# Loading v of row 1 earlier and placing row 1's values in the middle of chunk 0's second product

## The chip, the cores and the metric

The kernel runs on one core of a Trainium2 chip. The metric is the device time of one execution in microseconds (us). Three runs of the kernel before gave 306.92, 307.39 and 307.52; the median is 307.39. The profiled execution took 307.2 us, of which the span from the first to the last instruction is 305.4.

The engines named here are PE (TensorE: matmuls and transposes into PSUM), ACT (ScalarE), DVE (VectorE), POOL (GpSimd) and SP (SyncE, which only issues transfers). A transfer is issued by an engine and moved by the core's 16 DMA engines. Queue 0 of the profile carries what POOL issues, queue 1 what SP issues.

## What is computed

The program is windowed attention over 8 batches ("rows" in the kernel) with 8 heads each, followed by a feed-forward layer over all 4608 tokens.

```python
# q, k, v: (8, 8, 576, 64) float32;  w_in: (512, 2048);  w_out: (2048, 512)
scores = q @ k^T / 8
# heads 0-3 ("sliding"): key j is seen by query i if 0 <= i - j < 32
# heads 4-7 ("dilated"): 0 <= i - j < 128 and (i - j) % 4 == 0
attn = softmax(masked scores)
x = (attn @ v), heads side by side            # (4608, 512)
out = relu(x @ w_in) ** 2 @ w_out             # (4608, 512) float32
```

## The kernel before

The kernel interleaves two streams on PE. The feed-forward layer works on nine chunks of 512 tokens. Attention works on eight rows of 576 tokens and writes its result, transposed, into `xT`. While chunk c is multiplied, row c+1 goes through attention. The chunks are generators, and `pump(n)` lets the current one emit n further steps (two matmuls of the first product, and two matmuls of 512 columns in chunk 0's second product, or four or eight matmuls of 256 columns in the later ones). Between two calls of `pump` stands a piece of attention. Every engine executes its own instructions in the order in which they were written down, so the places of the `pump` calls decide what stands beside what.

Row 0 and the masks come first, together with short matmuls on zeros. Then these loads are issued for what follows. `landed` is a one-column copy on POOL that holds everything behind it on POOL until a transfer has arrived.

```python
load_w_out(0, 1)
landed(wi[:, NDM - 1, 1023:1024])
nc.gpsimd.memset(sq[:, :, :, 0:1], 0.0)
load_sliding_qk(1)              # SP: q, k of row 1, heads 0-3
load_dilated_qk(1)              # POOL: q, k of row 1, heads 4-7
load_w_out(1, 4)                # POOL: the other three quarters of w_out
landed(wo[:, 3, DM - 1 :])
nc.gpsimd.memset(sv[:, :, :, 0:1], 0.0)
nc.gpsimd.memset(sd[:, :, :, 0:1], 0.0)
load_v(1)                       # SP: six transfers into sv, two into sd
landed(wo[:, NFF - 1, DM - 1 :])
landed(sd[:, 1, HH - 1, DIL * D - 1 :])
dk = keep_qk(2)                 # POOL: q, k of row 2, DRAM to DRAM, to fp16
```

`keep_qk` writes row 2's q and k as fp16 into a DRAM tensor `dk`; later DMA transposes read it into `QKTx` and `QKTd`. Rows 2 to 7 get q and k in this way, row 1 through PE transposes (`pt`, `pd`).

Chunk 0 then goes through its two products. The second one goes four output tiles wide (`po_0` to `po_3`), a quarter of w_out at a time:

```python
g0 = hidden(0)
pending.append(mm1_gen(0, g0))
pump(28)
cast_sliding_qk(1, (nc.scalar, nc.vector, nc.scalar, nc.vector))
pump(1000)
pending.append(mm2_by_rows_gen(0, g0))
pump(1)
for hp in range(2):
    for i in (1, 0):
        t_sliding(1, hp, i, True)     # 6 transposes (pt) and a copy
        pump(1)
    if hp:
        for g in range(2):
            s_sliding(1, g)           # 12 score matmuls (ps), 2 exp, 2 masks
            pump(2)
for g in range(2):
    for i in (1, 0):
        t_dilated(1, g, i, True)      # 6 transposes (pd) and two copies
        pump(1)
scores_dilated(1, lambda: pump(3))    # twice: 16 score matmuls (pz), 2 exp, 2 masks
cast_v(nc.scalar)                     # ACT: sv -> vp, then sd -> vd (two instructions)
pump(2)
# ... rows_and_load: pump(1); after its second call row 2's DMA transposes and v
attn_values(1, rows_and_load, True)
pump(1000)
```

`attn_values` emits, with a call of its argument after each: three groups of sliding values (`pav`, 8 matmuls, then reciprocal and product on DVE), output transposes `px`, four groups of dilated values (`paw`), and output transposes `py`; the transposes are copied by ACT into `xT`. All of row 1's `pt`, `ps`, `pd`, `pz`, `pav`, `paw`, `px` and `py` tiles take turns in one PSUM pool of two buffers:

```python
papool = ctx.enter_context(tc.tile_pool(name="papool", bufs=2, space=bass.MemoryType.PSUM))
```

For rows 2 to 7 the loop over `b` emits chunk b-1 with row b inside it. In its first round (b = 2) it stores chunk 0, forms sums of w_out on DVE (`weight_sums`), and then:

```python
if b == 2:
    # ... stores of chunk 0
    dk = keep_qk(b + 1)
    for _ in weight_sums():
        pump(2)
    pump(2)
else:
    pump(11)
for g in range(2):
    s_sliding_x(b, g)
    pump(5)
s_dilated(b, 0)
pump(5 if b == 2 else 7)
s_dilated(b, 1)
# ... DMA transposes of row b+1
pump(2 if b == 2 else 6)
cast_v(nc.scalar)
# ... load_v(b + 1)
pump(5 if b == 2 else 3)
n_val[0] = 0
def rows():
    n_val[0] += 1
    pump(1 if b == 2 and n_val[0] > 7 else 2)
attn_values(b, rows)
pump(1000)
```

Of the kernel before, what the change touches and what calls it, by code (L numbers as in the profile page):

```python
# [17 lines left out]
def kernel(  # L18
# [9 lines left out]
    nc = tc.nc  # L28

    B, H, S, D = q.shape  # L30
    W = 32
    DIL = 4
    NTOK, DM = out.shape
    DFF = moe_w_in.shape[1]
    assert (B, H, S, D) == (8, 8, 576, 64) and DM == H * D and NTOK == B * S
    HH = H // 2
    NDM = DM // P
    NFF = DFF // P
# [8 lines left out]
    NB = S // QB  # L47
# [25 lines left out]
    wo = wpool.tile([P, NFF, DM], FP16, name="wo")  # L73
# [9 lines left out]
    sv = stg.tile([P, NB, HH, D], FP32, name="sv")  # L83
    sd = stg.tile([P, 2, HH, DIL * D], FP32, name="sd")
# [13 lines left out]
    def load_sliding_qk(b, engs=(nc.sync, nc.sync)):  # L98
        for i, src in enumerate((q, k)):
            engs[i].dma_start(  # L100
                out=sq[:, i, :, :],
                in_=src[b, 0:HH].rearrange("h (p j) d -> p h (j d)", j=6),
            )
# [17 lines left out]
    def load_sliding_v(b, m0=0, m1=NB):  # L121
        for m in range(m0, m1):
            lo = QB * m - PADP
            p0 = PADP if m == 0 else 0
            nc.sync.dma_start(
                out=sv[p0:P, m, :, :],
                in_=v[b, 0:HH, lo + p0 : lo + P, :].transpose([1, 0, 2]),
            )

    def load_dilated_v(b, eng, ts=(0, 1)):  # L130
        vv = v[b, HH:H].rearrange("h (i c) d -> i h (c d)", c=DIL)
        if 0 in ts:
            eng.dma_start(out=sd[PADD:P, 0, :, :], in_=vv[0:QD])
        if 1 in ts:
            eng.dma_start(out=sd[:, 1, :, :], in_=vv[QD - PADD : CL])

    def load_v(b):
        load_sliding_v(b)
        load_dilated_v(b, nc.sync)

    def load_dilated_qk(b):
        for i, src in ((1, k), (0, q)):
            s4 = src[b, HH:H].rearrange("(g e) (p j) d -> e p g (j d)", e=2, j=12)
            for e in range(2):
                nc.gpsimd.dma_start(out=nd_[48 * e : 48 * (e + 1), i, :, :], in_=s4[e])
# [18 lines left out]
    def copy(eng, o, i):  # L164
        if eng is nc.scalar:
            nc.scalar.copy(o, i)
        else:
            eng.tensor_copy(o, i)
# [26 lines left out]
    def cast_sliding_v(eng, step, m0=0, m1=NB):  # L195
        for m in range(m0, m1, step):
            copy(eng, vp[:, m : m + step, :, 0:D], sv[:, m : m + step, :, :])

    def cast_dilated_v(eng, step, ts=(0, 1)):
        for t in ts:  # L200
            for c in range(0, DIL, step):
                copy(
                    eng,
                    vd[:, t, c : c + step, :, 0:D],
                    sd[:, t, :, D * c : D * (c + step)].rearrange("p h (c d) -> p c h d", d=D),
                )

    def cast_v(eng):
        cast_sliding_v(eng, NB)
        cast_dilated_v(eng, DIL)  # L210
# [331 lines left out]
    def pump(n):  # L542
        for _ in range(n):
            while pending:
                try:
                    next(pending[0])
                    break
                except StopIteration:
                    pending.pop(0)


    def pa(name, dt=FP32):
        return papool.tile([P, 2, 512 if dt == FP32 else 1024], dt, name=name, tag="pa")
# [73 lines left out]
    def softmax(u, ps, mask):  # L627
        nc.scalar.activation(AT[:, u, 0:UW], ps[:, :, 0 : UW // 2], ACTF.Exp, scale=scale)  # L628
        nc.vector.tensor_mul(AT[:, u, 0:UW], AT[:, u, 0:UW], mask)  # L629

    def s_sliding(b, hp):
        tiles = [pa(f"ps{b}_{hp}_{half}") for half in range(2)]
        for half, ps in enumerate(tiles):
            for m3 in range(3):
                m = 3 * half + m3
                for e in range(2):
                    r = slice(D * e, D * (e + 1))
                    nc.tensor.matmul(  # L638
                        ps[:, e, QB * m3 : QB * (m3 + 1)],
                        QKTp[hp][r, 1, QB * m : QB * m + P],  # L640
                        QKTp[hp][r, 0, PADP + QB * m : PADP + QB * (m + 1)],
                        start=True,
                        stop=True,
                    )
        for half, ps in enumerate(tiles):
            softmax(2 * hp + half, ps, maskp)
# [19 lines left out]
    def s_dilated(b, g):  # L666
        tiles = [pa(f"pz{b}_{g}_{h}") for h in range(2)]
        for h, ps in enumerate(tiles):
            for a in range(2):
                for t in range(2):  # L670
                    q0 = KPAD + (2 * g + h) * CL + QD * t
                    for e in range(2):
                        r = slice(D * e, D * (e + 1))
                        n = 2 * a + t
                        nc.tensor.matmul(  # L675
                            ps[:, e, QD * n : QD * (n + 1)],
                            QKTd[r, 1, a, q0 - PADD : q0 - PADD + P],
                            QKTd[r, 0, a, q0 : q0 + QD],
                            start=True,
                            stop=True,  # L680
                        )
        for h, ps in enumerate(tiles):
            softmax(4 + 2 * g + h, ps, maskd)
# [148 lines left out]
    def scores_dilated(b, fill):  # L832
        for g in range(2):
            s_dilated(b, g)
            fill()

    def attn_values(b, fill, wide=False):
        xs = []
        for mp in range(3):
            xs += av_sliding(b, 2 * mp, 2 * mp + 2)  # L840
            fill()
        x_sliding(b, 0, xs, wide)
        fill()
        ys = av_dilated(b, 0, 0)
        fill()
        x_sliding(b, 1, xs, wide)
        fill()
        ys += av_dilated(b, 0, 1)
        fill()
        zs = []  # L850
        for a in range(2):
            zs += av_dilated(b, 1, a)
            fill()
        x_dilated(b, 0, ys, wide)
        fill()
        x_dilated(b, 1, zs, wide)
# [9 lines left out]
    def landed(x):  # L866

        nc.gpsimd.tensor_copy(hold[0 : x.shape[0]], x)
# [57 lines left out]
    landed(wi[:, NDM - 1, 1023:1024])  # L926
    nc.gpsimd.memset(sq[:, :, :, 0:1], 0.0)
    load_sliding_qk(1)
    load_dilated_qk(1)
    load_w_out(1, 4)  # L930
    landed(wo[:, 3, DM - 1 :])
    nc.gpsimd.memset(sv[:, :, :, 0:1], 0.0)
    nc.gpsimd.memset(sd[:, :, :, 0:1], 0.0)
    load_v(1)

    landed(wo[:, NFF - 1, DM - 1 :])
    landed(sd[:, 1, HH - 1, DIL * D - 1 :])
    dk = keep_qk(2)


# [7 lines left out]
    for hp in range(2):  # L948
        for i in (1, 0):
            t_sliding(1, hp, i, True)  # L950
            pump(1)
        if hp:
            for g in range(2):
                s_sliding(1, g)
                pump(2)
    for g in range(2):
        for i in (1, 0):
            t_dilated(1, g, i, True)
            pump(1)
    scores_dilated(1, lambda: pump(3))  # L960
    cast_v(nc.scalar)
    pump(2)
    n_val = [0]

    def reload_v(b):
# [16 lines left out]
    for b in range(2, B):  # L982
        pending.append(moe_gen(b - 1))
        pump(1)
        if b < B - 1:

            for i in range(2):
                nc.gpsimd.tensor_copy(hold, QKTx[:, i, PADP + HH * S - 2 : PADP + HH * S - 1])
                nc.gpsimd.tensor_copy(hold, QKTd[:, i, 1, KPAD + S - 1 :])
        if 2 < b < B - 1:  # L990
            dk = keep_qk(b + 1)
        if b == 2:
            for rows, ot in late:
                nc.gpsimd.dma_start(out=rows, in_=ot)
            dk = keep_qk(b + 1)
            for _ in weight_sums():
                pump(2)
            pump(2)
        else:
            pump(11)  # L1000
        for g in range(2):
            s_sliding_x(b, g)
            pump(5)
        s_dilated(b, 0)
        pump(5 if b == 2 else 7)
        s_dilated(b, 1)
        if b + 1 < B:
            transpose_by_dma(dk)
        pump(2 if b == 2 else 6)
        cast_v(nc.scalar)  # L1010
        if b + 1 < B:
            load_v(b + 1)
        pump(5 if b == 2 else 3)
        n_val[0] = 0

        def rows():
            n_val[0] += 1
            pump(1 if b == 2 and n_val[0] > 7 else 2)

        attn_values(b, rows)  # L1020
        pump(1000)
    for c in range(B - 1, NTOKC):
        pending.append(moe_gen(c))
# [31 lines left out]
```

The softmax here doesn't subtract the row's maximum and nothing guards it: scores larger than these inputs give would overflow.

## Time and profile before

| What | Value |
|---|---|
| time, median of 3 runs | 307.39 us |
| span of the profiled execution | 305.4 us |
| PE busy | 296.0 us, 97% of the span |
| DVE, ACT, POOL busy | 208.8, 185.0, 47.9 us |
| granted PE clock, mean | 0.999 |
| chunk 0's second product with row 1 | 38.44 to 62.53 us |
| chunk 1 with row 2 | 62.53 to 95.05 us |
| chunk 2 with row 3 | 95.19 to 126.08 us |

The busy time of an engine is the sum of its instructions; matmuls overlap in the array, so a busy PE is not PE at its peak. A line of the timeline gives the start, the time taken, the engine, the line of the kernel, the operation, output and input, and how many instructions are merged; in brackets stand the idle time before it and what ended it. SPq, POOLq and ACTq lines are issues of transfers: their time is that of issuing, not of moving. `L168` and `L166` are copy helpers, so the tiles tell what is copied.

### The profile page before, as it was taken

How to read it: one execution, taken by the hardware profiler on the slowest of the kernel's cores; microseconds unless marked ns; L12 is line 12 of the kernel's file. 1: busy time of each engine (PE TensorE's matmuls, PEld its weight loads, DVE VectorE, ACT ScalarE, POOL GpSimd, SP SyncE). 2: the span in 40 equal slices, each digit the busy share in tenths (PEclk: the TensorE clock that was granted, in tenths of full speed). 3: DMA queues.
4: the chain of work that ended last, by engine and by line, in shares of the span. 5: the costliest groups of instructions: out<-in, count | busy, mean ns of one | idle time of the engine just before them, and what ended most of it. 6: DMA issues, size and time to landing. Idle time of an engine off the chain costs nothing.

```text
span 305.4 us, 7012 instructions
## 1 busy us (share of the span) xinstructions
PE 296.0 (97%) x2898; PEld 192.3 (63%) x2898; DVE 208.8 (68%) x410; ACT 185.0 (61%) x308; POOL 47.9 (16%) x98
## 2 busy tenths in 40 slices
PE   7899999999998999999999999999999999999995
PEld 3675444544785469646974697459745974684484
DVE  4662474769974797679766977697769775834744
ACT  6567776668924893489348943894389536405710
POOL 7546000206004100320032003200100010000000
PEclk9999999999999999999999999999999999999999
DMA  8999996899989999999929983999320012003004
GB/s 176 227 212 232 236 208 145 155 194 208 314 178 251 267 154 178 267 196 197 230 103 205 203 188 126 217 191 205 115 73 0 2 54 85 2 0 137 2 0 138
DMA packets 85615, 47.89 MB, mean 157 GB/s; under 512 B 68112, under 2 KB 82896, under 8 KB 85200
## 3 DMA queue, kind: packets, MB, share of 16 engines
q1 hardware_dynamic: 76688, 27.24, 41.3%
q0 software_dynamic: 8352, 19.80, 29.2%
q8 instruction: 22, 0.36, 0.5%
q10 hardware_dynamic: 544, 0.43, 0.5%
q14 instruction: 9, 0.07, 0.1%
HBM read 39.85 MB, written 16.52 MB: 185 GB/s over the span
## 4 chain that ended last, share of the span: by engine, by line
PE 89%; DMA 3%; DVE 2%; ACT 2%; POOL 2%; issue 1%; ACTq 0%; POOLq 0%
PE ph L388 42%; PE poa L438 9%; PE pob L438 9%; PE pod L438 5%; PE poe L438 4%; PE poc L438 4%; PE po L409 3%; DMA early<-in_q_dram 3%; PE paw L776 2%; PE pav L759 2%; PE pz L675 2%; PE ps L656 1%; PE px L791 1%; PE py L809 1%; POOL early L119 1%; DVE x_d L740 1%
## 5 line engine op out<-in xcount | busy, mean ns | idle before, releaser
L388 PE MATMUL ph<-xT,wi 128*128 128x512 f16 x576 | 129.8, 380 | 0.3 <-ACT xT L815 0.3
L354 ACT ACTIVATE rt<-ph 128x512 f16<-128x512 f32 x144 | 84.9, 601 | 36.8 <-PE ph L388 36.4
L388 PEld LDWEIGHTS <-wi 128*128 128x128 f16 x576 | 54.4, 98 | 62.9 <-issue 0.6
L358 DVE TENSOR_TENSOR g<-rt 128x1024 f16<-128x1024 f16 x63 | 43.5, 691 | 45.5 <-ACT rt L354 45.2
L438 PEld LDWEIGHTS <-sm 128*128 128x128 f16 x512 | 46.8, 98 | 4.8
L438 PEld LDWEIGHTS <-g 128*128 128x128 f16 x384 | 36.0, 98 | 6.9 <-DVE g L356 1.3
L438 PE MATMUL pob<-T,sm 128*128 128x256 f16 x256 | 32.8, 272 | 0.0
L438 PE MATMUL poa<-wo,g 128*128 128x256 f16 x256 | 32.6, 273 | 0.0
L458 POOL DMA_DIRECT2D out_dram<-otl x6 | 4.6, 761 | 148.4 <-DVE otl L493 131.1
L815 ACT COPY xT<-py 128x576 f16<-128x576 f16 x16 | 10.2, 638 | 25.5 <-PE py L809 25.4
L740 DVE TENSOR_TENSOR x_d<-paw,rcp_d 72x512 f16<-72x512 f32 x32 | 22.0, 687 | 1.1
L797 ACT COPY xT<-px 128x576 f16<-128x576 f16 x16 | 10.3, 642 | 14.0 <-PE px L791 14.0
L628 ACT ACTIVATE AT<-pz 128x576 f16<-128x576 f32 x28 | 16.7, 649 | 1.9 <-PE pz L675 1.5
L409 PE MATMUL po<-wo,g 128*128 128x512 f16 x64 | 17.8, 380 | 0.0
L628 ACT ACTIVATE AT<-ps 128x576 f16<-128x576 f32 x28 | 16.7, 650 | 0.8 <-PE ps L638 0.4
L740 DVE TENSOR_TENSOR x_p<-pav,rcp_p 96x512 f16<-96x512 f32 (+1 forms) x24 | 16.2, 676 | 0.8
L735 DVE RECIPROCAL rcp_d<-paw 72x8 f32<-72x8 f32 x32 | 6.3, 198 | 15.1 <-PE paw L776 15.1
L438 PE MATMUL poe<-wo,sm 128*128 128x256 f16 x128 | 16.5, 273 | 0.0
L438 PE MATMUL poc<-T,sm 128*128 128x256 f16 x128 | 16.4, 272 | 0.0
L438 PE MATMUL pod<-T,g 128*128 128x256 f16 x128 | 16.1, 273 | 0.0
L629 DVE TENSOR_TENSOR AT<-AT,maskp 128x576 f16<-128x576 f16 x28 | 12.7, 457 | 2.8 <-ACT AT L628 1.9
L478 ACT COPY otu<-poa 128x512 f32<-128x512 f32 x8 | 4.7, 586 | 16.1 <-PE poa L438 16.1
(120 smaller groups left out, 352.6 us busy)
## 6 DMA issues: line engine op xcount, KB each, us to landing
sv<-in_v_dram SPq DMA_DIRECT2D x40, 128.0 KB, 4.6
sd<-in_v_dram SPq DMA_DIRECT2D x8, 512.0 KB, 6.8
dk<-in_k_dram POOLq DMA_DIRECT2D x12, 288.0 KB, 6.3
dk<-in_q_dram POOLq DMA_DIRECT2D x12, 288.0 KB, 7.8
out_dram<-otl POOLq DMA_DIRECT2D x6, 512.0 KB, 3.3
out_dram<-otu POOLq DMA_DIRECT2D x6, 512.0 KB, 4.6
sd<-in_v_dram SPq DMA_DIRECT2D x8, 288.0 KB
wi<-in_moe_w_in_dram POOLq DMA_DIRECT2D x4, 512.0 KB, 10.6
```

Source lines behind the costliest of these rows:

```text
L354: nc.scalar.activation(rt[:, o, :], ph[:], ACTF.Relu)
L358: nc.vector.tensor_mul(g[:, ffc - 1 : ffc + 1, :], rt, rt)
L388: nc.tensor.matmul(ph, wi[:, dmk, ffc * P : ffc * P + P], xs[:, dmk, :], start=(n == 0), stop=(n == NDM - 1),)
L409: nc.tensor.matmul(po, g[:, ffc, t * P : (t + 1) * P], wo[:, ffc, :], start=(ffc == 0), stop=(ffc == NFF - 1),)
L438: nc.tensor.matmul(acc, lhs[:, k, t * P : (t + 1) * P], rhs[:, k, :], start=(first and k == 0), stop=(k == NK - 1), skip_group_check=True,)
L628: nc.scalar.activation(AT[:, u, 0:UW], ps[:, :, 0 : UW // 2], ACTF.Exp, scale=scale)
L629: nc.vector.tensor_mul(AT[:, u, 0:UW], AT[:, u, 0:UW], mask)
L675: nc.tensor.matmul(ps[:, e, QD * n : QD * (n + 1)], QKTd[r, 1, a, q0 - PADD : q0 - PADD + P], QKTd[r, 0, a, q0 : q0 + QD], start=True, sto ...
L735: nc.vector.reciprocal(rcp[0:w, 0:n], pv[:, :, :, D])
L740: nc.vector.tensor_tensor(out=x[0:w, 0:n], in0=pv[:, :, :, 0:D], in1=rcp[0:w, 0:n].unsqueeze(3).to_broadcast([w, n, HH, D]), op=ALU.mult,)
L797: nc.scalar.copy(xT[:, 0:2, t0 : t0 + 288], px[:, 0:UW].rearrange("x (c t) -> x c t", c=2),)
L815: nc.scalar.copy(xT[:, 2:4, t0 : t0 + 288].rearrange("x c (i r) -> x c i r", r=DIL), py[:, 0:UW].rearrange("x (c r i) -> x c i r", c=2, r= ...
```

## The change

The loads of row 1's v are issued directly behind those of its sliding q and k, on SP. The two waits for w_out, the wait for v, and the two memsets that held v's load are gone, so `keep_qk(2)` follows w_out on POOL without a hold. In chunk 0's second product the fillers between the pieces of row 1's attention are cut, so that its values come in the middle of the product and the rest of the product comes after them; the cast of the sliding v moves ahead of the dilated scores. In chunk 1 the fillers are placed anew around row 2. The purpose is to have the values of row 1, and row 2's transposes behind them, done sooner.

```diff
     load_sliding_qk(1)
+    load_v(1)
     load_dilated_qk(1)
     load_w_out(1, 4)
-    landed(wo[:, 3, DM - 1 :])
-    nc.gpsimd.memset(sv[:, :, :, 0:1], 0.0)
-    nc.gpsimd.memset(sd[:, :, :, 0:1], 0.0)
-    load_v(1)
-
-    landed(wo[:, NFF - 1, DM - 1 :])
-    landed(sd[:, 1, HH - 1, DIL * D - 1 :])
     dk = keep_qk(2)
@@ row 1 in chunk 0's second product
             t_sliding(1, hp, i, True)
             pump(1)
-        if hp:
-            for g in range(2):
-                s_sliding(1, g)
-                pump(2)
+    for g in range(2):
+        s_sliding(1, g)
+        pump(1)
     for g in range(2):
         for i in (1, 0):
             t_dilated(1, g, i, True)
-            pump(1)
-    scores_dilated(1, lambda: pump(3))
-    cast_v(nc.scalar)
-    pump(2)
+    cast_sliding_v(nc.scalar, NB)
+    scores_dilated(1, lambda: pump(1))
+    cast_dilated_v(nc.scalar, DIL)
@@ row 2 in chunk 1, and the later rows
             for _ in weight_sums():
                 pump(2)
-            pump(2)
@@
             s_sliding_x(b, g)
-            pump(5)
+            pump(7 if b == 2 and g else 5)
@@
-        pump(5 if b == 2 else 3)
-        n_val[0] = 0
-
-        def rows():
-            n_val[0] += 1
-            pump(1 if b == 2 and n_val[0] > 7 else 2)
-
-        attn_values(b, rows)
+        pump(4 if b == 2 else 3)
+        attn_values(b, lambda: pump(2))
         pump(1000)
```

In instructions: PE, ACT, DVE and SP execute as many as before, in another order; POOL has five fewer. On PE the order of chunk 0's second product becomes: the first half of it spread over row 1's scores and values as before but more thinly, and after the last output transpose (`py_1`) 26 of its 64 matmuls in one piece. On ACT, `vp<-sv` stands ahead of the four `AT<-pz`, and the four copies of `po` to the output tile follow the copies of `py`. In chunk 1 the last output transpose is followed directly by chunk 2's first matmul, where one half product (8 matmuls) stood between them before.

## Prediction

> **What bounds the kernel now.** I read the page first, then busy time in 10 us stretches, then the timeline of the stage that the diff edits, then the DMA records packet by packet. From the page:
>
> ```profile
> span 305.4 us, 7012 instructions
> ...
> PE 296.0 (97%) x2898; PEld 192.3 (63%) x2898; DVE 208.8 (68%) x410; ACT 185.0 (61%) x308; POOL 47.9 (16%) x98
> ...
> PE 89%; DMA 3%; DVE 2%; ACT 2%; POOL 2%; issue 1%; ACTq 0%; POOLq 0%
> ```
>
> TensorE is the bound: 97% busy and 89% of the chain that ended last. Busy time by stretch (length, then PE, PEld, DVE, ACT, POOL, clock, DMA share, GB/s):
>
> ```profile
> 40.00:50.00 10.00, 9.49 (x107) 4.99 (x107) 5.94 (x14) 6.35 (x13) 0.18 (x1) 1.00 1.09 201
> 50.00:60.00 10.00, 9.46 (x114) 4.87 (x113) 5.97 (x17) 6.79 (x9) 2.18 (x5) 1.00 0.61 122
> 60.00:70.00 10.00, 9.71 (x61) 4.33 (x58) 7.39 (x14) 6.80 (x12) 0.39 (x1) 1.00 1.03 201
> ...
> 90.00:100.00 10.00, 8.74 (x79) 5.37 (x77) 5.92 (x12) 4.11 (x7) 4.02 (x9) 1.00 1.11 265
> ```
>
> Only chunk 0's second product with row 1 (38.4 to 62.5) and the end of chunk 1 (near 93) have gaps; from 100 us PE is full. The busy figure hides part of the gap. Bare costs: 13.81 us for the 64 matmuls of 512 columns of chunk 0's first product, so 0.216 each; a group of six transposes or eight value matmuls takes 0.26 start to start when nothing holds it, a score group of 12 or 16 takes 0.36. The stage is 64 x 0.216 + (8 transpose + 7 value + 4 output-transpose groups) x 0.26 + 4 x 0.36 = 13.8 + 4.9 + 1.4 = 20.2 us. It takes 62.53 - 38.44 = 24.1. So the most that a better order can win here is about 3.9 us, 1.3%. The timeline of the stage:
>
> ```profile
> 35.24 8.90 SPq L125 DMA_DIRECT2D sv<-in_v_dram  x6
> ...
> 44.24 1.81 SPq L133 DMA_DIRECT2D sd<-in_v_dram  x1
> ...
> 48.05 0.70 ACT L166 COPY QKTd<-pd 128x288 f16<-128x288 f16 x2 [0.89 <-PE pd L577]
> ...
> 48.72 1.19 ACT L628 ACTIVATE AT<-pz 128x576 f16<-128x576 f32 x2
> ...
> 51.86 1.47 ACT L166 CAST vp<-sv 128x1536 f16<-128x1536 f32 x1
> ...
> 53.22 2.00 ACT L166 CAST vd<-sd 128x1024 f16<-128x1024 f32 x2
> 53.38 0.42 PE L759 MATMUL pav<-vp,AT 128*128 128x65 f16 x8 [0.25 <-ACT vp L166]
> ...
> 53.54 0.18 POOL L868 COPY hold<-sd 128x1 f32<-128x1 f32 x1 [5.66 <-DMA sd<-in_v_dram]
> 54.03 0.54 POOL L220 DMA_DIRECT2D dk<-in_k_dram  x1 [0.31 <-issue]
> ...
> 62.53 8.36 PE L388 MATMUL ph<-xT,wi 128*128 128x512 f16 x38 [0.29 <-ACT xT L815]
> ```
>
> Here v is cast only after all exponentials of row 1, its load lands by 53.5, and only then do the four dk copies of row 2 begin. Values cost PE a short wait for the cast; the end of the stage waits for the last xT copy.
>
> **What the Trainium skill says.** "DMA: Bandwidth & Descriptors", section "Queues, rings and completion order": each DMA engine goes round robin, packet by packet, between the queues that have work. Counting this trace's records agrees: from 39 to 44 us queue 0 (w_out, 1024 B) moved 149 to 154 packets a us and queue 1 (v, 256 B) 147 to 184, though v got only a fifth of the bytes. Same page, "Issuing engines are not separate DMA queues": issuing from several engines saves only issue time, the transfers interleave. So v on SyncE's queue isn't put ahead of w_out on GpSimd's. "TensorE: Matmul & The Clock Gate", section "Architectural detail": ACT and DVE are strict FIFO, and PE may only pull weight loads ahead. The order of the ACT program therefore decides; in the trace weight loads do start ahead of a held matmul (one value weight load at 52.76, its matmul at 53.38).
>
> **Part 1, the loads.** Issue of v moves from 35.24 to about 24.6, behind q k of row 1 on one queue. But that queue is busy with q k until 35.5 to 36 (packets of 1536 B end there). So v's data start near 36 instead of 38.6: a gain of about 2.5 us, not 11. From 36, w_out has some 1450 packets left; at 150 a us they last to about 45.5, and v gets about 9.5 x 150 = 1430 of its 2944 packets of 256 B (6 tiles) by then. Its 800 packets of 1024 B (sd) stand behind.
>
> **Part 2, dk unheld.** dk's four copies now follow w_out on GpSimd's queue at once and reach the engines near 45.5, just when v had the engines alone before (486, then 904 packets in the two us from 44). dk is 64 packets of 18432 B. In rows 2 to 7, alone, they pass at 11 to 12 a us, 5.5 to 6 us in all. Beside them v is nearly stopped: from 103 to 107 us 44 dk packets went with 154 packets of sd, 3.5 to one. So over dk's 6 to 7 us (45.5 to 52) v gets about 64 x 3.5 = 220 packets; 1290 are left, at 700 to 900 a us 1.7 us. The sv tiles then land at about 53.5 to 54.5 (before: about 48.5), sd at 160 to 215 a us some 4 to 5 us after, near 58.
>
> **Part 3, the order on ACT and PE.** The cast of sv now stands ahead of row 1's four dilated exponentials on ACT. The attention PSUM pool has two buffers, so the second pair of scores needs the first exponential done, and the first value group the third. Also four transpose groups follow each other with no filler matmul, each needing a buffer from a copy. Walk it, from 41.98 which is unchanged. First score pair 42.51, second 43.6 and 44.1; its exponentials end 44.63 and 45.23. Transpose groups pd at 44.75 and 45.3; their copies (DVE after two masks) end 46.57 and 46.45; next two pd 46.6 and 46.9; copies end 47.86 and 48.0. First two pz at 47.9 and 48.1, filler to 48.7. If sv had landed, ACT casts it 48.0 to 49.47 and the exponentials end at 50.07, 50.66, 51.26, 51.85. So pz of the second pair is at 50.1 and 50.7, the first values at 51.35. From there to the last output transpose the steps go at the pace of DVE's 0.20 + 0.69 and of ACT's copies: py of the second half at about 59.8. Then 26 filler matmuls of 0.216 = 5.6, and chunk 1 begins at about 65.7, where before it was 62.5. Order alone: +3.2 us. With sv landing at 54.2 in place of 48.0 everything from the cast on shifts by 6.2 us, as PE has no other work that stands ahead of it: +9.4 in all. The sd cast then comes at 58, about when it lands, so it adds 0 to 1.
>
> **Part 4, chunk 1.** Before: its last output transpose waits for DVE until 94.01, 1.2 us. After: a half product more stands before it, so that wait goes to near 0. But the half product that followed it is gone, and chunk 2's first matmul needs the ACT copy of that transpose; at 61.37 to 62.53 this took 1.16 us, 0.26 of it work, so 0.9 of new wait. Later chunks take 30.9 us each, chunk 1 takes 95.05 - 62.53 = 32.5; I count -0.4 net. The final xT wait of chunk 0 (0.6 us) is already within part 3. Sum: 307.4 + 9.4 - 0.4 = 316.4. Removing five small GpSimd waits is worth nothing by itself, since no PE wait goes through them but those told.
>
> **Rivals.** (a) v gets through. If the copies start later than I think, or share engines evenly by bytes with v, sv lands by 48 to 50, and only the order costs: +3 to +5, 310.5 to 312. For: dk took 8 us rather than 6 at 54, so it is not always greedy. Against: 103 to 107 us. (b) As designed: v is early enough, values come mid product, the fillers at the end hide the last copy, and most of the 3.9 us of gaps goes: 304.5 to 306. For: no xT wait at 62.5, and row 2's transposes earlier. Against: row 2's keys landed at 68.4 and were wanted at 70.8, so that is no wait now; and 26 fillers at the end stand idle where row 1 has gaps. (c) The starved sd adds its own wait after sv: 318 to 320.
>
> **Range and chances.** Main path 316.4 with some 60%, (a) 30%, (b) and (c) the rest; I put the middle at 315.5. The range 309.5 to 319 covers (a)'s upper part and (c). The 2% line above is 313.5, between (a) and the main path: slower 0.65, within 0.33, faster 0.02 (6.1 us is more than all gaps of both stages).
>
> **What would show it.** ACT's cast of sv beginning at 53 to 55 and ended by DMA sv, with PE idle of 6 to 9 us between 45 and 58 while dk's queue is full: right. Cast near 48: part 2 wrong, (a). First matmul of chunk 1 near 71 to 72: sum right; 65 to 66: order alone; before 62.5: (b), part 3 wrong. Chunk 2's first matmul should wait about 0.9 us for the xT copy. Chunks 2 to 8 must keep 30.9 and 26.0 us.

## The result and the profile after

The changed kernel takes 320.69 us (median of four runs, 319.0 to 321.51) against 307.44 us for the kernel before (four runs, 306.92 to 307.52). The ratio is 1.0428, with a 95% interval of 1.0383 to 1.0472: slower by 13.2 us. The prediction had the direction right and was 5.2 us too low; the measured time lies 1.7 us above its range.

From the page of the changed kernel:

```profile
span 319.2 us, 7004 instructions
...
PE 300.5 (94%) x2898; PEld 195.0 (61%) x2898; DVE 208.7 (65%) x410; ACT 185.4 (58%) x308; POOL 46.8 (15%) x93
...
PEclk9999995599999999999999999999999999999999
...
PE 82%; DMA 5%; SPq 5%; ACT 3%; DVE 3%; issue 1%; ACTq 0%
```

The span grew by 13.8 us and PE's busy time by 4.5, though PE executes the same 2898 matmuls: some of them ran more slowly. The row of the granted clock says which: two of its forty slices, from about 48 to 64 us, show half of full speed. In the chain that ended last, 5% is now a DMA and 5% SyncE's queue.

Busy time of the changed kernel by 10 us stretch (length, then PE, PEld, DVE, ACT, POOL, clock, DMA share, GB/s):

```profile
40.00:50.00 10.00, 7.59 (x95) 4.13 (x94) 5.62 (x13) 5.28 (x11) 0.00 (x0) 0.88 1.21 218
50.00:60.00 10.00, 1.44 (x18) 0.81 (x18) 1.33 (x3) 3.63 (x6) 0.00 (x0) 0.50 1.10 200
60.00:70.00 10.00, 9.77 (x97) 5.32 (x95) 6.67 (x19) 3.60 (x6) 0.74 (x4) 0.76 1.05 222
70.00:80.00 10.00, 10.00 (x54) 4.68 (x54) 2.70 (x5) 5.50 (x10) 3.52 (x6) 1.00 0.56 167
```

PE did 1.44 us of work between 50 and 60, where it did 9.46 before. After that it is full again, but until 64.7 us at half clock, so "9.77 busy" is not 9.77 us of progress. The timeline of the changed kernel names the wait:

```profile
24.74 18.60 SPq L125 DMA_DIRECT2D sv<-in_v_dram  x6
...
36.66 0.52 POOL L220 DMA_DIRECT2D dk<-in_q_dram  x1 [0.81 <-DMA early<-in_k_dram]
...
47.33 0.70 ACT L166 COPY QKTd<-pd 128x288 f16<-128x288 f16 x2 [0.76 <-PE pd L577]
...
48.55 1.04 PE L409 MATMUL po<-wo,g 128*128 128x512 f16 x2
...
56.37 1.47 ACT L166 CAST vp<-sv 128x1536 f16<-128x1536 f32 x1 [8.34 <-DMA sv<-in_v_dram]
57.75 2.35 ACT L628 ACTIVATE AT<-pz 128x576 f16<-128x576 f32 x4
58.45 0.96 PE L675 MATMUL pz<-QKTd 64*128 64x72 f16 x16 [8.86 <-ACT AT L628]
```

ACT stood 8.34 us in front of the cast of sv. The exponentials stood behind the cast, and PE's next score groups (`pz`) stood behind those: 8.86 us. Chunk 1 began at 75.90 instead of 62.53, so 13.4 of the 13.8 us are lost by then.

### The profile page after: what moved, and what is told of

Read it like the earlier page. It is cut to its first block, busy times and chain, and to the rows that moved or that the text cites. A ratio compares the mean times of both kernels' runs of the same rounds, so it can differ in the third digit from the quotient of the medians.

```text
span 319.2 us, 7004 instructions
## 1 busy us (share of the span) xinstructions
PE 300.5 (94%) x2898; PEld 195.0 (61%) x2898; DVE 208.7 (65%) x410; ACT 185.4 (58%) x308; POOL 46.8 (15%) x93
## 4 chain that ended last, share of the span: by engine, by line
PE 82%; DMA 5%; SPq 5%; ACT 3%; DVE 3%; issue 1%; ACTq 0%
PE ph L388 35%; PE pob L438 9%; PE poa L438 9%; DMA sv<-in_v_dram 5%; SPq L125 5%; PE poe L438 4%; PE pod L438 4%; PE poc L438 4%; PE po L409 4%; PE pj L538 3%; PE paw L776 2%; PE pav L759 2%; PE pz L675 1%; PE ps L656 1%; PE py L809 1%; PE px L791 1%
## 5 line engine op out<-in xcount | busy, mean ns | idle before, releaser
L815 ACT COPY xT<-py 128x576 f16<-128x576 f16 x16 | 10.2, 638 | 28.5 <-PE py L809 28.5
L629 DVE TENSOR_TENSOR AT<-AT,maskd 128x576 f16<-128x576 f16 x28 | 12.3, 455 | 11.6 <-ACT AT L628 10.7
L409 PE MATMUL po<-wo,g 128*128 128x512 f16 x64 | 19.4, 419 | 0.0
L675 PE MATMUL pz<-QKTd 64*128 64x72 f16 x224 | 6.7, 203 | 9.6 <-ACT AT L628 8.9
```

Source lines behind the costliest of these rows:

```text
L409: nc.tensor.matmul(po, g[:, ffc, t * P : (t + 1) * P], wo[:, ffc, :], start=(ffc == 0), stop=(ffc == NFF - 1),)
L675: nc.tensor.matmul(ps[:, e, QD * n : QD * (n + 1)], QKTd[r, 1, a, q0 - PADD : q0 - PADD + P], QKTd[r, 0, a, q0 : q0 + QD], start=True, sto ...
L815: nc.scalar.copy(xT[:, 2:4, t0 : t0 + 288].rearrange("x c (i r) -> x c i r", r=DIL), py[:, 0:UW].rearrange("x (c r i) -> x c i r", c=2, r= ...
```

## The experiments

Times of the kernel before, in the three sessions: 307.47, 307.11 and 307.31 us. The ratios are against those of the same session.

The theory was that v is starved by row 2's unheld copies, on top of a dearer order on ACT and PE. The first rival was that the order alone does it; later ones were the granted clock and the size of the copies' packets.

**The held copies (e1_dk_held).** The changed kernel, with row 2's `dk` copies held again until row 1's v has landed.

```diff
     load_w_out(1, 4)
+    landed(sd[:, 1, HH - 1, DIL * D - 1 :])
     dk = keep_qk(2)
```

> The changed kernel with one line back: row 2's dk copies are held until row 1's v has landed. Theory (dk's 18 KB packets stop v's 256 B packets): v has the engines alone from about 45.5 us, the sv tiles land near 48, the ACT cast of sv begins at 48 to 49 in place of 56.4, PE's idle stretch shrinks from 9 to under 2 us, chunk 1 begins near 66; 310 to 312.5 us. Rival (the new order on ACT and PE costs it, whatever the loads do): 317 to 321. Rival (v is slow because it now meets w_out from the start): sv still lands after 53; 316 to 319.

Measured 315.12 us, ratio 1.0246 (1.0229 to 1.0264). Holding the copies gives back 5.6 us, so they do cost what the theory says. But what is left, 7.7 us over the kernel before, is far more than the order was expected to cost, and the time lies in none of the three ranges. The cast of sv began at 51.13, not at 48 to 49. Here v is issued from 25.57 on, where the kernel before issues it from 35.24 on, and yet its last transfer is complete only at 50.90, against 50.78 in the kernel before: the earlier issue by itself brought nothing.

**The loads alone (e2_loads_only).** The kernel before, with only the new block of loads.

```diff
     load_sliding_qk(1)
+    load_v(1)
     load_dilated_qk(1)
     load_w_out(1, 4)
-    landed(wo[:, 3, DM - 1 :])
-    ...                     # two memsets, load_v(1), two more holds
     dk = keep_qk(2)
```

> The kernel before with the new loads alone: v behind q k on SP, no holds, dk at once; PE and ACT order as before. Theory: sv lands near 56 as in the changed kernel, but the dilated exponentials stand ahead of the cast, so PE waits from about 52.4 to 58 at the first values (5.6 us of which 0.4 were there before), plus some at half clock: 312 to 315 us. Rival (order alone): 307 to 308.

Measured 312.15 us, ratio 1.0153 (1.0136 to 1.017). The loads cost 4.7 us even in the old order. (One of the four runs took 318.06 us at a lower granted clock throughout; it is left out of the ratio.) That is less than the 5.6 us in the new order. A reason is that in the old order ACT did the exponentials first and reached the cast only at 51.86 in the kernel before, so that part of the delay of v was hidden.

**The order alone (e3_order_only).** The changed kernel with the old block of loads put back.

```diff
     load_sliding_qk(1)
-    load_v(1)
     load_dilated_qk(1)
     load_w_out(1, 4)
+    landed(wo[:, 3, DM - 1 :])
+    ...                     # two memsets, load_v(1), two more holds
     dk = keep_qk(2)
```

> The changed kernel with the old loads and holds back; order of row 1 and row 2 new. Theory: sv lands near 48.5 as before, the cast begins there, chunk 1 begins near 66 (3.3 us later than before) plus 0 to 1 for sd, which landed at 53.5, plus 0.4 in chunk 1: 310.5 to 313 us. Rival (order costs all): 318 to 321. Rival (order is good, only the loads hurt): 304.5 to 307.5.

Measured 315.14 us, ratio 1.0252 (1.0237 to 1.0267): above the theory's range and below the first rival's, and 7.7 us over the kernel before. ACT's timeline of this kernel:

```profile
50.30 1.47 ACT L166 CAST vp<-sv 128x1536 f16<-128x1536 f32 x1 [2.46 <-DMA sv<-in_v_dram]
51.68 2.35 ACT L628 ACTIVATE AT<-pz 128x576 f16<-128x576 f32 x4
```

and its busy time in 2 us stretches, columns as above:

```profile
46.00:48.00 2.00, 0.91 (x27) 0.76 (x27) 1.22 (x4) 1.08 (x4) 0.18 (x1) 1.00 0.82 191
48.00:50.00 2.00, 0.86 (x15) 0.28 (x8) 0.00 (x0) 0.00 (x0) 0.00 (x0) 0.62 0.79 202
50.00:52.00 2.00, 0.00 (x0) 0.00 (x0) 0.00 (x0) 1.70 (x2) 0.00 (x0) 0.50 0.38 129
...
56.00:58.00 2.00, 2.00 (x14) 0.90 (x12) 1.55 (x6) 0.00 (x0) 0.00 (x0) 0.50 0.79 166
```

Two things are seen here that the walk did not have. Even by the old loads v is there only at 50.3, not at 48.0. And the clock column falls to 0.50 and stays there until after 58, with PE full at 56 to 58. From the start of the cast to chunk 1's first matmul it takes 69.83 - 50.30 = 19.53 us, where 17.7 had been walked. It is 19.53 in the changed kernel (75.90 - 56.37) and 19.52 in e1_dk_held, so this is one fixed piece.

**The cast behind the scores (e4_cast_behind).**

```diff
-    cast_sliding_v(nc.scalar, NB)
     scores_dilated(1, lambda: pump(1))
-    cast_dilated_v(nc.scalar, DIL)
+    cast_v(nc.scalar)
```

> The changed kernel with the cast of sv put behind the four dilated exponentials, loads as changed. Theory: sv still lands near 56, exponentials and the second pair of dilated scores are out of the way by 52, and the first values follow the cast at once, about 58 instead of 60.2; half clock stays: 317.5 to 319.5 us. Rival (the cast's place ahead of the exponentials is the main cost): 311 to 313.

Measured 317.82 us, ratio 1.0339 (1.0323 to 1.0354). Doing the exponentials during the wait takes 2.9 us off the changed kernel. The cast still waits for v and begins at 55.76, against 56.37, so its place is not the main cost.

**Chunk 1 alone (e5_chunk1_only).** The kernel before with only the new fillers of chunk 1.

```diff
-            pump(2)             # after the weight sums
...
-            pump(5)
+            pump(7 if b == 2 and g else 5)
...
-        pump(5 if b == 2 else 3)
-        ...                     # rows(): one or two fillers
+        pump(4 if b == 2 else 3)
+        attn_values(b, lambda: pump(2))
```

> The kernel before with the new fillers of chunk 1 alone. From the changed kernel's trace (chunk 1 took 32.96 us there, 32.52 before): +0.4, 307.6 to 308.2 us, with the wait of chunk 2's first matmul for the xT copy near 0.7 us. Rival, the step of my prediction: -0.4, 306.8 to 307.2.

Measured 307.72 us, ratio 1.0015 (1.0007 to 1.0024): a small loss where a small gain had been predicted. PE's timeline of this kernel at the end of chunk 1:

```profile
94.03 0.29 PE L809 MATMUL py<-ident,x_d 72*128 72x72 f16 x4
94.62 0.30 PE L809 MATMUL py<-ident,x_d 72*128 72x72 f16 x4 [0.30 <-DVE x_d L740]
95.65 5.34 PE L388 MATMUL ph<-xT,wi 128*128 128x512 f16 x24 [0.73 <-ACT xT L815]
```

The last transpose still waits 0.30 us for DVE, and the wait of chunk 2 for `xT` (0.73) has come on top. A third one, 0.30 us, is that of row 2's values for the cast of v (at 82.47). In the changed kernel the same waits stand at 107.83, 108.86 and 95.68, with 0.30, 0.73 and 0.30. In all PE stands idle for 1.41 us of chunk 1 in this kernel and in the changed one, and for 1.26 us in the kernel before.

**Chunk 1 as the later chunks (e6_chunk1_as_later).** As e5_chunk1_only, but with `pump(5)` after both sliding scores as in the later rows, so that the two fillers go to the end of the chunk.

> The kernel before with chunk 1's fillers set so that row 2's pieces meet the products where rows 3 to 7 meet theirs (a half product after the last output transpose, and the third value group before the end of the fourth product). If the gap at the end of chunk 1 comes only from DVE's order there: 306 to 306.8 us. If DVE is behind because of the weight sums, the wait only moves: 307.2 to 308.5.

Measured 305.6 us, ratio 0.9953 (0.9936 to 0.997), below both ranges. Chunk 1 takes 30.98 us (62.35 to 93.33), the pace of the later chunks. The last transpose begins at 92.17 without a wait, eight matmuls follow it from 92.43 on, and chunk 2 begins at 93.33 without a wait. So a filler block after the last transpose covers the `xT` copy, and the place of two fillers is worth 1.9 us between e5 and e6.

**A filled wait (e7_filled).** The changed kernel with `pump(13)`, 26 matmuls, in place of `pump(1)` between the two pairs of dilated scores; 24 of them come from the end of the stage.

```diff
-    scores_dilated(1, lambda: pump(1))
+    n_fill = iter((13, 1))
+    scores_dilated(1, lambda: pump(next(n_fill)))
```

> The changed kernel, loads and all, with 24 of the 26 matmuls of 512 columns that stood after row 1's last output transpose put between the two pairs of dilated scores, where PE stood idle for 9 us. Theory (PE is idle because its own program has nothing there, and half clock follows from the idle time): 5.2 us of work go into the gap and 0 to 1.8 us of half clock with them: 312.5 to 315.8 us. Rival (the stage's end is set by row 1's chain of copies and loads, not by PE's order): 318 to 321.

Measured 314.79 us, ratio 1.0246 (1.0223 to 1.0269): by the two ratios 5.6 us come back. Its busy time in 4 us stretches shows how the clock behaves:

```profile
44.00:48.00 4.00, 2.36 (x44) 1.64 (x39) 3.07 (x8) 2.73 (x7) 0.00 (x0) 1.00 1.26 244
48.00:52.00 4.00, 4.00 (x26) 1.62 (x27) 0.00 (x0) 0.00 (x0) 0.00 (x0) 0.57 0.92 198
52.00:56.00 4.00, 3.75 (x18) 1.57 (x17) 0.00 (x0) 0.60 (x1) 0.00 (x0) 1.00 1.46 238
```

Here PE is full from 48.3 on, and yet the clock is at half until 51.7. So a long wait didn't cause that drop. It follows the thin stretch from 44 to 48, in which four transpose groups stand one behind another without fillers and PE was busy for 2.36 of 4 us. After 3.4 us of full work the clock is whole again. It falls once more from 58.5 to 62.0, behind a wait of 1.72 us for the exponentials.

**The wait kept busy (e12_busy_wait).** e3_order_only, with the first pair of dilated score groups of row 1 computed five times (64 more small matmuls, the same values). That puts work in front of the wait, and changes nothing on the path after the cast.

```diff
-        for h, ps in enumerate(tiles):
+        again = 5 if (b, g) == (1, 0) else 1
+        for h, ps in list(enumerate(tiles)) * again:
```

> The order-only kernel (e3, 315.1 us) with row 1's first pair of dilated score groups computed five times over into the same PSUM tiles, where PE stood idle from 48.9 to 52.4: useless work in idle time, same result. Theory (half clock after the idle stretch costs about 1.8 us in the values that follow): the clock is back at full by 53, the stage ends 1.3 to 2 us earlier: 313 to 314 us. Rival (the values are slow for another reason): 315 or more.

Measured 313.34 us, ratio 1.022 (1.0181 to 1.0259). Three of the four runs took 313.07 to 313.37 us, the fourth 316.31; the intervals of this and of e3 overlap, so the times alone don't settle it. The trace says more. Its busy time by stretch:

```profile
50.00:52.00 2.00, 0.20 (x8) 0.19 (x8) 0.22 (x1) 2.00 (x3) 0.00 (x0) 1.00 0.38 87
52.00:54.00 2.00, 1.77 (x26) 1.05 (x19) 1.61 (x4) 2.00 (x4) 1.31 (x3) 0.65 0.00 0
54.00:56.00 2.00, 2.00 (x15) 0.90 (x13) 1.47 (x4) 1.25 (x2) 1.01 (x3) 0.50 0.96 147
56.00:58.00 2.00, 1.71 (x25) 1.07 (x24) 1.27 (x5) 0.64 (x1) 0.00 (x0) 1.00 1.36 285
```

The half clock lasts 3.4 us instead of ten. The clock now stays whole at the place of the old drop, where the added matmuls stand, and falls only at 52.6, behind the wait. So the expectation that it would be back by 53 was wrong: it had not fallen before. The piece from the cast to chunk 1 takes 68.28 - 49.73 = 18.55 us instead of 19.53. So 1.0 of the 1.8 us beyond the walk goes with the half clock that is gone.

**Smaller packets for dk (e11_dk_2k).** The changed kernel, with row 2's copies in pieces of 2048 B instead of 18432 B.

```diff
...                             # o and s_ are the copy's output and input
+                if b == 2:
+                    o = o.rearrange("(a b x) -> b a x", b=16, x=1024)
+                    s_ = s_.rearrange("(a b x) -> b a x", b=16, x=1024)
```

> The changed kernel with row 2's dk copies written in packets of 2048 B instead of 18432 B, nothing else. Theory (turns are taken by packet, and 18 KB packets are what stops v): while dk passes, v gets 80 packets a us or more instead of 20 to 50, the sv tiles land 1.5 to 3 us earlier than in the changed kernel (cast at 53.4 to 55), 317.5 to 319.5 us. Rival (dk takes its share by bytes or comes first whatever its packets): cast at 56 to 57, 320 to 321.5.

Measured 320.32 us, ratio 1.0422 (1.0408 to 1.0437), the same as the changed kernel; the expectation of a gain fell. Beside the small packets v did get 83 to 118 packets a us (46 to 52 us) instead of 18 to 50. But the copies then kept taking their turns until 53.5, where nearly all of the large packets had begun by 51, and the cast began at 55.66, 0.7 earlier. What costs the time is that the copies run beside v at all, as e1_dk_held shows, and not the size of their packets.

**v first, cast on GpSimd (e8_v_first).** The kernel before, with chunk 1 as in e6. v goes right behind q k of row 1, and now the second half of w_out is held until sv has landed; GpSimd casts v.

```diff
     load_sliding_qk(1)
-    load_dilated_qk(1)
-    load_w_out(1, 4)
-    ...                     # holds and memsets
     load_v(1)
-    ...                     # holds
+    load_dilated_qk(1)
+    load_w_out(1, 2)
+    landed(sv[:, NB - 1, HH - 1, D - 1 :])
+    load_w_out(2, 4)
+    cast_v(nc.gpsimd)
     dk = keep_qk(2)
...
-    cast_v(nc.scalar)
-    pump(2)
```

> The aim of the change by other means: v behind q k on SP, the last two quarters of w_out held until sv has landed, v cast by GpSimd (which holds dk behind v too), row 1's order as before but with the two fillers ahead of the values moved to the end, chunk 1 as in e6. Theory: v alone from about 39 us, sv lands at 42 to 44, sd at 46 to 48, w_out's last quarter by 51; the waits for the sv cast (0.4), for the xT copy behind the casts (0.5) and for the last xT copy (0.5) go: 304.8 to 306.5 us. Rival (w_out now late: PE waits for its third quarter near 51): 307.5 to 311.

Measured 309.8 us, ratio 1.0085 (1.0062 to 1.0109), a miss. v did land early: GpSimd's hold on sv passed at 44.01. The time lies in the rival's range, but what held PE was not w_out. The timeline of this kernel:

```profile
45.23 4.85 DVE L629 TENSOR_TENSOR AT<-AT,maskp 128x576 f16<-128x576 f16 x2 [0.57 <-ACT AT L628]
...
45.95 1.50 POOL L168 CAST vp<-sv 128x1536 f16<-128x1536 f32 x1
...
47.36 2.03 POOL L168 CAST vd<-sd 128x1024 f16<-128x1024 f32 x2
...
50.87 0.66 PE L577 MATMUL pd<-ident,early 96*128 96x96 f16 x6 [3.89 <-DVE QKTd L168]
```

One of DVE's mask products took 4.49 us; the others took 0.45. It ended when GpSimd's three casts had ended, DVE's next copies came late by as much, and PE waited 3.89 us for one of them. By this trace the product began at 45.23, 0.7 us ahead of the first cast and so longer than it takes alone; times on GpSimd are rough, so which of the two was first isn't shown. That the casts are the cause is borne out by the next run, in which they stand on ACT and no mask product of this stage took over 0.46 us.

**v first, cast on ACT (e9_v_first_act).** As e8_v_first, but the copies of row 2 wait for sd, and the casts stay on ACT. Those of sv go in two halves between the groups of transposes.

```diff
-    cast_v(nc.gpsimd)
+    landed(sd[:, 1, HH - 1, DIL * D - 1 :])
     dk = keep_qk(2)
...
             t_dilated(1, g, i, True)
             pump(1)
+        cast_sliding_v(nc.scalar, 3, 3 * g, 3 * g + 3)
     scores_dilated(1, lambda: pump(3))
+    cast_dilated_v(nc.scalar, DIL)
```

> As e8, but v is cast by ACT again and dk is held by a one-column copy of sd: the sv cast in two halves, one behind each pair of dilated transposes where ACT had 0.9 us of idle time, the sd cast behind the dilated exponentials. Theory (in e8 GpSimd's 3.5 us of casts held DVE's mask product for 4.4 us; the loads themselves were good, sv landed by 44): no gap near 48, PE at full clock, and the three waits of e8's expectation go: 303.8 to 305.3 us. Rival (the held w_out is late, or the halves delay the exponentials): 306 to 309.

Measured 304.86 us, ratio 0.9927 (0.9913 to 0.9941): faster than both kernels, with chunk 1 as in e6 and the two fillers ahead of the values moved to the end of the stage. Its timeline:

```profile
47.66 0.84 ACT L166 CAST vp<-sv 128x768 f16<-128x768 f32 x1
...
49.26 0.85 ACT L166 CAST vp<-sv 128x768 f16<-128x768 f32 x1
```

Neither cast waits for a load.

**The fillers alone (e10_fillers).** e6_chunk1_as_later without the `pump(2)` ahead of row 1's values (those fillers fall to the end of the stage). It helps to tell what part of e9 is owed to v.

> The kernel before with chunk 1's fillers as in e6 (305.6 us) and the two fillers ahead of row 1's values moved behind its last output transpose; loads and casts as before. Theory: of the waits, the one for the last xT copy (0.5) goes, the one for the sv cast grows by up to 0.4 to 0.9, so nothing much is won without the loads: 305.2 to 306.2 us.

Measured 306.05 us, ratio 0.9963 (0.9949 to 0.9976). Here PE waits 1.11 us for the cast of sv. Against e9 that leaves 1.2 us for early v together with its holds and its earlier casts, and the two intervals don't meet. But e10 is by the medians 0.4 us slower than e6, which keeps these two fillers where they were, so e6 is the fairer mark: against it e9 is 0.7 us faster, and those intervals just overlap. In the traces, one execution each, chunk 0's second product takes 24.09 us in the kernel before and in e6, 24.50 in e10 and 23.98 in e9, and chunk 1 takes 30.98 in all three against 32.52. So most of what e9 wins comes from chunk 1's fillers. What early v wins is small, and a gain over e6 is not shown.

## Why the prediction was right and wrong

Three steps failed. The landing of v: "1290 are left, at 700 to 900 a us 1.7 us" puts the cast of sv at 54.2, and it began at 56.37, 2.2 us later. The walk from this cast to chunk 1: it has no term for the clock, and took 1.8 us longer. In chunk 1, "that wait goes to near 0": it did not, and with the wait for `xT` this makes 0.8 us. Together that is the 4.8 us by which the predicted 9.0 us fall short of the 13.8 measured.

**Parts 1 and 2, the loads: right in what happens, right in the difference, wrong in both landings.** Counted from the DMA records of the changed kernel:

| packets a us, from | 45 | 46 | 47 | 48 | 49 | 50 | 51 | 52 | 53 | 54 | 55 |
|---|---|---|---|---|---|---|---|---|---|---|---|
| dk, 18432 B | 9 | 6 | 12 | 13 | 10 | 10 | 1 | 3 | 0 | 0 | 0 |
| sv, 256 B | 134 | 41 | 50 | 27 | 22 | 18 | 460 | 548 | 122 | 116 | 7 |
| sd, 1024 B | 0 | 0 | 0 | 0 | 0 | 0 | 0 | 62 | 209 | 191 | 212 |

(In the last column 234 packets of 256 B passed; only 7 of v's 2944 were left, so the others are taken to be those of row 2's transposes.) v had moved 1399 packets by 45 (predicted 1430 by 45.5), got 292 beside dk (predicted 220), and had 1253 left at 51 (predicted 1290). The step that failed is the next. The rest took about 5 us. After two full microseconds sv's packets trickle at 116 to 122 a us while sd's, issued behind them, already move; so the cast began at 56.37 instead of 54.2. The completion counts in the trace show the tail too. Of the 16 counts of the last transfer into sv, twelve came by 53.55, the other four at 54.63, 55.44, 55.62 and 56.14. The Trainium skill says what they count ("DMA: Bandwidth & Descriptors", section "Why a DMA increments its semaphore by 16 and not by 1"): a DMA runs on up to 16 engines that finish independently, and only the full count means that all has landed. So four counts came late, and a mean rate of all engines doesn't give the landing. The records don't name the engines; why these were behind stays open.

The old loads have the same tail: in e3_order_only 938 and 540 packets of 256 B a us at 45 and 46, then 159 and 53; twelve counts of the last transfer by 47.34, the other four at 47.78, 47.91, 48.34 and 50.05, and the cast at 50.30. The prediction read "before: about 48.5". In the timeline of the kernel before nothing shows this landing, since ACT reached the cast only at 51.86. But its DMA records do. The prediction quotes 486 and 904 packets; the next four us have 418, 210, 91 and 12, and the last count came at 50.78. That the two misreadings cancel in the difference is luck: 56.37 - 50.30 = 6.07 us against 6.2 predicted.

**Part 3, the order: the mechanism right, its size not.** "If sv had landed, ACT casts it 48.0 to 49.47" failed, as sv lands at 50.3 even by the old loads: 2.3 us. And the prediction had no term for the clock: 19.53 us from cast to chunk 1, not 17.7, makes 1.8 us; e12_busy_wait takes 1.0 of them back. One stretch of PE's program, from the first sliding value group (`pav`) to the first dilated one (`paw`), is the same in the kernel before and in the changed one. The kernel before reaches its end at:

```profile
56.81 0.41 PE L776 MATMUL paw<-vd,AT 128*128 128x65 f16 x8 [0.29 <-ACT xT L797]
```

The changed kernel has:

```profile
60.17 0.65 PE L759 MATMUL pav<-vp,AT 128*128 128x65 f16 x8
...
65.46 0.41 PE L776 MATMUL paw<-vd,AT 128*128 128x65 f16 x8 [0.23 <-ACT xT L797]
```

That is 56.81 - 53.38 = 3.43 us before and 65.46 - 60.17 = 5.29 after, and also 5.29 in e3_order_only: 1.86 us more. In e12_busy_wait, where only the first 2.6 us of it are at half clock, it is 4.43. The Trainium skill speaks of this ("TensorE: Matmul & The Clock Gate", section "A second HAM failure mode: psum-queue depth-cycling"): short idle times between groups of matmuls are enough to make the clock alternate between half and full. The trace of e7_filled agrees, with 2.36 us busy of 4 and then 0.57.

**Part 4: wrong in its sign.** Predicted -0.4, measured +0.44: chunk 1 takes 108.86 - 75.90 = 32.96 us, before 32.52. The new wait for `xT` came (0.73, predicted 0.9). But "that wait goes to near 0" failed: a wait of 0.30 for DVE stayed, and one of 0.30 for the cast of v was new.

**The sum.** Of the span's 13.8 us: order as walked 3.2, v's real landing by the old loads 2.3, half clock 1.8, the new loads 6.07, chunk 1 0.44. The first and the fourth were predicted (the 3.2 is the walk's own figure; e3_order_only measures it together with the next two). The others, and the -0.4 that was counted for chunk 1, make the error against the 9.0 predicted.

**Rivals and chances.** Rival (a), that v gets through, had pulled the middle below the sum and set the low end of the range. It was wrong in itself: with dk held the time is 315.12, not 310.5 to 312, since landing and clock cost their 4.1 us there too. Rival (b), the design's intent, failed on the loads and on the order. In e9_v_first_act, where w_out and dk are held back and half of sv's cast goes between the transposes, v is early, and even there the stage is only 0.1 us shorter than in the kernel before. Rival (c), sd's own wait, didn't come: both casts of sd begin right behind the exponentials. The bet on slower (0.65) was right, though the size came out larger than any path that was written down.

## What to carry to other kernels

An early issue is not an early landing: ask which queue and which engines the load shares, and what the removed waits now let run beside it. On an engine that runs in order, put no work that waits for a load ahead of work that frees the next engine's buffers. And where program order hides a load's landing from the timeline, read it from the queue's packets to the last one and from the completion counts, not from a mean rate.

## What the runs showed of the hardware

- The tail of a load: in e3_order_only 1478 packets of sv passed in two us and the last 212 took two more; the last completion count came another 1.1 us later (50.05).
- TensorE's granted clock changed in steps, by the clock records of all traces but e2_loads_only's. The stretches at half clock last 3.4 us in e12_busy_wait, 6.8 in e8_v_first, 10.2 in e1_dk_held and e3_order_only, 13.7 in e4_cast_behind and e11_dk_2k and 17.1 in the changed kernel, all multiples of 3.41 us. Counted in such steps, between 30 and 110 us, the clock fell after each in which PE was busy for 64% or less (64% in the changed kernel, 56% in e3 and e7) and after none with 70% or more (70% in e5, 74% in e12). It came back only after a step that was full; 84% was not enough in e1. Near the ends of the kernels steps of 42 to 59% kept the clock, so the share of busy time alone is not the rule.
- GpSimd casting in SBUF held a DVE product of two SBUF operands for 4.49 us instead of 0.45. The Trainium skill ("SBUF — State Buffer", section "SBUF: two separate sides") calls the ports that the two share an exclusive lock for one whole instruction. Here the wait ended only behind three GpSimd instructions, of 1.50 us and of 2.03 us for two. Why DVE didn't get in between them was not tried.
